# Side work between MoE items, three units' squares on GpSimd, and two reciprocal transfers for four

## The chip, the cores and the metric

One core of a Trainium2 chip runs the whole kernel. The metric is the device time in microseconds (us) of one execution. A kernel is timed in rounds, on the same chip as the kernel before, and the two are compared round by round.

Engines: TensorE (PE in the profile, its weight loads PEld), VectorE (DVE), ScalarE (ACT), GpSimd (POOL), SyncE (SP), whose queue issues most DMAs.

## The reference, cut to what matters

Attention with normalized q and k, 8 batches of 12 heads, 448 tokens, head size 64; its output goes through a two-layer block of width 2048 with a leaky ReLU, which the kernel calls MoE.

```python
def rmsnorm(x, g):
    rms = np.sqrt(np.mean(x * x, axis=-1, keepdims=True) + 1e-06)
    return x / rms * g
# ... q_n, k_n = normalized q, k; scores, softmax (exp, divided by the row sums), times v
h = x @ w_in                  # x: 3584 x 768, w_in: 768 x 2048
g = np.maximum(0.01 * h, h)
return (g @ w_out)            # w_out: 2048 x 768
```

## The kernel before

A unit is four heads of one batch, so there are 24 units and three to a batch. Each unit has four steps, d0 to d3. A step issues scores (`qk`), their exp (`ex`), some side work, and then `fill`, which hands out MoE items from a queue to keep TensorE busy. An item is six first-layer matmuls with a leaky ReLU on ScalarE (`moe1`), or eight second-layer matmuls (`moe2`). The items of a batch are pushed in step d3 of the unit after its last one; the first batch's are pushed early, in unit 2.

The side work of unit u prepares unit u + 2 (squares, sums, inverse norms, norms, a transpose by DMA) and finishes unit u - 1: a reciprocal of the softmax sums on ScalarE, spread over partitions by DMAs into `rz`, and a product on GpSimd that gives `xt`, the input of the first layer.

```python
def zcol_inv(u):                       # reciprocal of the softmax sums
    nc.scalar.activation(s["zs"], s["zs"], AF.Ln)
    nc.scalar.activation(s["zs"], s["zs"], AF.Exp, bias=0.0, scale=-1.0)
    # ...
    for r in range(2):
        for a in range(2):
            src = s["zs"][32 * a + 16 * r:32 * a + 16 * r + 16, None, :]
            nc.sync.dma_start(s["rz"][64 * a:64 * a + 64, r], src.broadcast_to([16, 4, S]))

# in the loop over units u and steps d  (cut)
    ex(u)
    if d == 0:
        # ...
        elif narrow(u - 1):
            zcol_inv(u - 1)            # ScalarE, then SyncE's queue
        # ...
        if u + 4 < NU:
            load(u + 4)                # q and k, 448 KB each, SyncE's queue
        if u + 2 < NU:
            prep_qg(u + 2, nc.gpsimd)
        if u + 3 < NU:
            load_v(u + 3)              # v, 224 KB, issued by GpSimd
        if 3 < u < NU - 2:
            prep_sq(u + 2)             # squares of q and k, ScalarE
    if d == 1 and u > 3 and narrow(u - 1):
        xmul_pool(u - 1)               # the product on GpSimd
    # ... d == 1: sums of squares; d == 2: inverse norms, norms, transpose
    fill(u, d)
```

## Time and profile before

| | |
|---|---|
| time | 452.05 us, 3 runs (451.57 to 452.19); later rounds gave medians of 451.8 to 452.6 |
| span of the profiled run | 450.6 us |
| 12 first-layer matmuls at the second batch's start | 3.45 us (2.37 undisturbed) |
| a unit in the steady part | 16.87 us |
| reciprocal DMAs | 76 of 112 KB, 3.3 us each from issue to landing |

The prediction below shows the lines of the page and of the timeline that carry its argument. What TensorE waits for from 50 us to 440 us stands in the list of waits (engine and line, what it waited for, total us, times, longest us):

```profile
PE sT L179 <- ACT et L198: 5.4, 8, 1.2
...
PE hps L325 <- POOL xt L290: 0.9, 1, 0.9
```

The first line is scores that wait for exp to free a PSUM slot, the second the second batch's first item, which waits for the product on GpSimd.

One more view of the kernel before matters afterwards: how the second batch's wait comes about, in the timeline of unit 6 (start, duration, engine, line, operation; SPq and POOL L106 rows are issues of DMAs):

```profile
93.96 0.76 POOL L106 DMA_DIRECT2D vt<-in_v_dram  x1
...
97.17 0.58 ACT L278 ACTIVATE zs<-zs 64x448 f32<-64x448 f32 x1
97.77 2.92 SPq L283 DMA_DIRECT2D rz<-zs  x4
100.79 0.55 SPq L103 DMA_DIRECT2D rq<-in_q_dram  x1
...
103.62 2.96 POOL L290 TENSOR_TENSOR xt<-x,rz 128x896 f16<-128x896 f32 x1 [8.89 <-ACT rinv L145]
...
106.63 1.67 PE L325 MATMUL hps<-xt,win 128*128 128x448 f16 x8 [0.92 <-POOL xt L290]
```

The load of v is issued 3.8 us before the reciprocal's DMAs, the load of q after them. The reciprocal ends on ScalarE at 97.74, its last DMA lands at 103.36 (5.6 us later, by the trace's record of arrivals), the product follows. (Its bracket names ScalarE's `rinv`, which it doesn't read: that update merely came last.)

### The profile page before, as it was taken

The numbers are of one execution on the slowest core, as the hardware profiler recorded it, in microseconds if no ns is written. First come the engines' busy times: TensorE is split into PE (matmuls) and PEld (weight loads), VectorE is DVE, ScalarE is ACT, GpSimd is POOL, SyncE is SP. The second block draws the span as 40 slices with busy tenths as digits, with TensorE's granted clock in tenths as the row PEclk, the third lists the DMA queues.
The fourth block names the chain that finished last, engine by engine and source line by source line (L and its number), as shares of the span: only waits on it lengthen the run. The fifth ranks groups of instructions, "written<-read, shape, count | busy, mean of one in ns | idle before, by whom it ended". The sixth has DMA issues, their size and how long they took to land.

```text
span 450.6 us, 8689 instructions
## 1 busy us (share of the span) xinstructions
PE 422.9 (94%) x3608; PEld 214.2 (48%) x3608; DVE 216.7 (48%) x320; ACT 313.2 (70%) x464; POOL 142.1 (32%) x96
## 2 busy tenths in 40 slices
PE   6668898889999999999999999999999999999995
PEld 6234343444445544455455544455455544555563
DVE  4688744576354564366354564366354540311011
ACT  5878688866985778966985778966984868444300
POOL 5878333145225135225225135225224101010000
PEclk9578999999999999999999999999999999999999
DMA  8999993777656866677567775587564441321022
GB/s 267 233 242 249 233 213 83 165 124 190 164 92 146 228 131 142 142 141 204 129 97 154 216 135 141 139 149 197 128 99 101 92 92 27 51 61 36 0 71 70
DMA packets 68586, 62.82 MB, mean 139 GB/s; under 512 B 38084, under 2 KB 63428, under 8 KB 68548
## 3 DMA queue, kind: packets, MB, share of 16 engines
q1 hardware_dynamic: 58272, 50.48, 46.3%
q0 software_dynamic: 10272, 11.80, 17.4%
q8 instruction: 28, 0.46, 0.4%
q14 instruction: 10, 0.08, 0.0%
q10 hardware_dynamic: 4, 0.00, 0.0%
HBM read 45.61 MB, written 11.01 MB: 126 GB/s over the span
## 4 chain that ended last, share of the span: by engine, by line
PE 68%; ACT 17%; DVE 7%; DMA 4%; issue 1%; POOL 1%; SPq 1%; DVEq 0%; POOLq 0%
PE op L340 30%; PE hps L325 20%; ACT et L198 7%; PE sT L179 6%; PE sT L310 5%; ACT sq L126 4%; PE zc L255 3%; ACT gt L327 3%; DMA rq<-in_q_dram 2%; ACT zs L277 1%; DVE zs L272 1%; DVE zs L273 1%; DVE ssq L139 1%; ACT zs L278 1%; DMA out_dram<-ost 1%
## 5 line engine op out<-in xcount | busy, mean ns | idle before, releaser
L198 ACT ACTIVATE et<-sT,eb 128x896 f16<-128x896 f32 x166 | 158.3, 1005 | 35.8 <-PE sT L179 25.6
L325 PE MATMUL hps<-xt,win 128*128 128x448 f16 x768 | 154.6, 353 | 2.9 <-DVE xt L319 1.0
L340 PE MATMUL op<-wout,gt 128*128 128x384 f16 x896 | 154.1, 326 | 0.0
L340 PEld LDWEIGHTS <-gt 128*128 128x128 f16 x896 | 84.4, 98 | 65.0 <-issue 11.9
L325 PEld LDWEIGHTS <-win 128*128 128x128 f16 x768 | 72.3, 98 | 74.4 <-issue 12.1
L290 POOL TENSOR_TENSOR xt<-x,rz 128x896 f16<-128x896 f32 x19 | 41.1, 2161 | 202.5 <-DMA rz<-zs 155.2
L327 ACT ACTIVATE gt<-hps 128x448 f16<-128x448 f32 x128 | 63.7, 538 | 21.0 <-PE hps L325 20.4
L134 POOL TENSOR_TENSOR qg<-rq,ggb 128x896 f32<-128x896 f32 (+2 forms) x25 | 64.3, 2573 | 36.5 <-DVE n L151 32.2
L151 DVE TENSOR_TENSOR n<-qg,rinv 128x896 f16<-128x896 f32 (+2 forms) x25 | 31.8, 1276 | 81.0 <-issue 32.9
L179 PE MATMUL sT<-qkT 64*64 64x448 f16 x664 | 54.2, 372 | 11.0 <-ACT et L198 10.5
L139 DVE TENSOR_REDUCE ssq<-sq 128x14 f32<-128x896 f32 (+2 forms) x49 | 50.1, 1061 | 28.9 <-ACT sq L126 28.9
L344 DVE COPY ost<-op 128x384 f32<-128x384 f32 x56 | 30.0, 551 | 58.5 <-PE op L340 58.5
L267 ACT COPY x<-sT 128x896 f32<-128x896 f32 x19 | 17.2, 905 | 32.5 <-PE sT L310 32.5
L179 PEld LDWEIGHTS <-qkT 64*64 64x64 f16 x672 | 15.8, 105 | 47.8 <-issue 44.3
L216 DVE TENSOR_REDUCE sT<-sT 128x1 f32<-128x896 f32 x22 | 24.1, 1095 | 29.0 <-PE sT L179 28.9
L151 DVE TENSOR_TENSOR n<-rk,rinv 128x896 f16<-128x896 f32 (+2 forms) x25 | 29.8, 1195 | 0.0
L310 PE MATMUL sT<-et,vt 64*64 64x448 f16 x532 | 28.5, 349 | 0.3
L310 PEld LDWEIGHTS <-vt 64*64 64x64 f16 x672 | 20.8, 109 | 12.0 <-issue 2.8
L126 ACT ACTIVATE sq<-rq 128x896 f32<-128x896 f32 (+2 forms) x22 | 19.7, 902 | 2.0 <-DMA rq<-in_q_dram 2.0
L126 ACT ACTIVATE sq<-rk 128x896 f32<-128x896 f32 x20 | 18.7, 935 | 0.0
L106 POOL DMA_DIRECT2D vt<-in_v_dram x24 | 18.4, 765 | 0.0
L255 PE MATMUL zc<-et,onesr 128*32 128x448 f16 (+1 forms) x304 | 16.1, 332 | 0.0
(60 smaller groups left out, 191.1 us busy)
## 6 DMA issues: line engine op xcount, KB each, us to landing
rq<-in_q_dram SPq DMA_DIRECT2D x24, 448.0 KB, 4.8
rk<-in_k_dram SPq DMA_DIRECT2D x24, 448.0 KB, 5.4
out_dram<-ost SPq DMA_DIRECT2D x56, 192.0 KB, 4.6
rz<-zs SPq DMA_DIRECT2D x76, 112.0 KB, 3.3
vt<-in_v_dram POOLq DMA_DIRECT2D x24, 224.0 KB, 5.5
win<-in_moe_w_in_dram POOLq DMA_DIRECT2D x8, 384.0 KB, 12.3
wout<-in_moe_w_out_dram POOLq DMA_DIRECT2D x2, 1536.0 KB, 22.1
qkT<-n SPq DMA_TRANSPOSE x19, 4.0
```

What stands on the lines that cost most here:

```text
L126: nc.scalar.activation(buf(u, "sq")[:, ti, :, c[0]:c[1]], raw[u][ti][:, :, c[0]:c[1]], AF.Square)
L134: eng.tensor_tensor(buf(u, "qg")[:, :, c[0]:c[1]], raw[u][0][:, :, c[0]:c[1]], ggb[:, None, None, :].broadcast_to([P, 2, n, D]), op=ALU.mult)
L139: nc.vector.tensor_reduce(buf(u, "ssq")[:, ti, :, c[0]:c[1]], buf(u, "sq")[:, ti, :, c[0]:c[1]], axis=AXL.X, op=ALU.add)
L151: nc.vector.tensor_tensor(buf(u, "n16")[:, ti, c[0]:c[1]].rearrange("p s a d -> p a s d"), src[:, :, c[0]:c[1]], buf(u, "rinv")[:, ti, :, ...
L179: nc.tensor.matmul(banks[a][64 * r:64 * r + 64, 0:S].rearrange("p (t x) -> p t x", t=NS), kT(u, r, a, t), qT(u, r, a), start=True, stop=True)
L198: nc.scalar.activation(s["et"][:, t], sT[:, :, 0:S], AF.Exp, bias=s["eb"], scale=1.0)
L290: nc.gpsimd.tensor_tensor(xts[b][:, g], s["x32"], s["rz"], op=ALU.mult)
L310: nc.tensor.matmul(s["pv"][r][64 * a:64 * a + 64, 0:S], vts[u % NV][64 * r:64 * r + 64, a, t], s["et"][64 * r:64 * r + 64, t, a], start=(t ...
L325: nc.tensor.matmul(hps[:, 0:S], win16[:, kt // 2, kt % 2, ts(ft, P)], xt[:, kt // 2, kt % 2], start=(kt == 0), stop=(kt == KT - 1))
L327: nc.scalar.activation(gt[:, ft, ds(S * (b % 2), S)], hps[:, 0:S], AF.Prelu, bias=0.0, scale=1.0, alpha=0.01)
L340: nc.tensor.matmul(op2[:, 0:HC], gt[:, ft, ts(t, P)], wout16[:, ft, ds(HC * half, HC)], start=(ft == 0), stop=(ft == FT - 1))
L344: nc.vector.tensor_copy(ost[0][:, ds(HC * half, HC)], op2[:, 0:HC])
```

## The change

Its intent: ScalarE and VectorE did a unit's side work in one piece ahead of the items, which held up exps and the emptying of PSUM. The change hands the pieces out one by one between items, takes the squares of units 6 to 8 off ScalarE, and halves the number of reciprocal DMAs by interleaving the rows of the sums.

```diff
-        nc.vector.memset(onesr[64 * r:64 * r + 64, 16 * r:16 * r + 16], 1.0)
+        nc.vector.memset(onesr[64 * r:64 * r + 64].rearrange("p (i r) -> p r i", r=2)[:, r], 1.0)
 ...
-            for a in range(2):
-                src = s["zs"][32 * a + 16 * r:32 * a + 16 * r + 16, None, :]
-                nc.sync.dma_start(s["rz"][64 * a:64 * a + 64, r], src.broadcast_to([16, 4, S]))
+            src = s["zs"][r:64:2, None, :]
+            nc.sync.dma_start(s["rz"][:, r], src.broadcast_to([32, 4, S]))
 ...                                          (in fill, behind each item)
+            if jobs:
+                jobs.pop(0)()
+        for job in jobs:
+            job()
 ...                                          (in the loop)
-                        zcol_inv(u - 1)
+                        job(zcol_inv, u - 1)
 ...
-                    if 3 < u < NU - 2:
-                        prep_sq(u + 2)
+                    if 6 < u < NU - 2:
+                        for ti in range(2):
+                            job(prep_sq, u + 2, ALL, (ti,))
 ...
+                if u < 6 and d == 2:
+                    prep_sqp(u + 3)                      # squares on GpSimd
 ...                                          (sums, inverse norms, norms, transpose: job(...) too)
-                fill(u, d)
+                fill(u, d, jobs)
```

Not shown in the cut: `pv_out`, a copy on ScalarE, and `zcol_sum` on VectorE change places.

More of the change, by code (lines that the diff above doesn't have):

```diff
@@ L372, in fed, with fill @@
         return u % NQ == 0 and d == 3
-    def fill(u, d):
+    def fill(u, d, jobs):
         total = sum(c for c, _ in queue)
@@ L531 @@
                             shift_mm(u)
+                            pv_out(u - 1)
                             zcol_sum(u - 1)
-                            pv_out(u - 1)
                         else:
@@ L539, with job @@
                     ex(u)
+                jobs = []
+                def job(fn, *args):
+                    jobs.append(lambda: fn(*args))
                 if d == 0:
@@ L566 @@
                     if d == 1:
-                        prep_ssq(u + 2)
+                        for ti in range(2):
+                            job(prep_ssq, u + 2, ALL, (ti,))
                     if d == 2:
-                        prep_rinv(u + 2)
-                        prep_norm(u + 2)
-                        prep_trd(u + 2)
-                fill(u, d)
+                        job(prep_rinv, u + 2)
+                        for ti in range(2):
+                            job(prep_norm, u + 2, ALL, (ti,))
+                        job(prep_trd, u + 2)
+                fill(u, d, jobs)
         zsum_slot(NU - 1)
```

## The prediction

> **What bounds the kernel now.** I read the page first, then the timeline unit by unit, then the chain of waits for the rates of undisturbed matmuls, and last the waits and the places where transfers land. A unit is four heads of one batch; each has four steps (d0 to d3): scores into PSUM, their exp on ScalarE, then some MoE items that fill TensorE meanwhile.
>
> ```profile
> PE 422.9 (94%) x3608; PEld 214.2 (48%) x3608; DVE 216.7 (48%) x320; ACT 313.2 (70%) x464; POOL 142.1 (32%) x96
> ...
> PE   6668898889999999999999999999999999999995
> ...
> ACT  5878688866985778966985778966984868444300
> POOL 5878333145225135225225135225224101010000
> ```
>
> TensorE is the bound. Its idle time lies in the first ten slices (11.3 us each), so to 113 us; behind it the row shows nines to the end. The page's busy time hides small stalls, though, so I compare the starts of successive blocks of matmuls in the timeline with undisturbed rates. These are at the end of the chain of waits, where nothing disturbs them:
>
> ```profile
> 406.46 18.16 PE hps L325 x96
> 424.62 20.81 PE op L340 x128
> ```
>
> That is 0.189 us for a first-layer matmul (an item of 6: 1.13 us) and 0.163 us for a second-layer one (an item of 8: 1.30 us). A pair of score steps, 8 matmuls, takes 0.51 us from its start to the next block's in undisturbed places (198.42 to 198.93), and a block of 16 second-layer matmuls with its switch 2.70 us (198.93 to 201.63). What blocks take beyond that is what any better order could win. From 45 us on it is 12.9 us in sum: about 9.0 us between 45 and 115 us (units 3 to 7), and about 3.9 us, in pieces of 0.1 to 0.5 us, from there to the end. The start-up before 45 us isn't touched by the change. The largest pieces all look like this one, in unit 6 (timeline: start, duration, engine, line, operation, and in brackets idle time with its releaser):
>
> ```profile
> 95.25 1.01 ACT L198 ACTIVATE et<-sT,eb 128x896 f16<-128x896 f32 x1 [0.55 <-DVE eb L226]
> ...
> 96.62 2.77 PE L340 MATMUL op<-wout,gt 128*128 128x384 f16 x16
> 97.17 0.58 ACT L278 ACTIVATE zs<-zs 64x448 f32<-64x448 f32 x1
> 97.65 0.94 ACT L126 ACTIVATE sq<-rq 128x896 f32<-128x896 f32 x1
> ...
> 98.49 0.93 ACT L126 ACTIVATE sq<-rk 128x896 f32<-128x896 f32 x1
> ...
> 99.33 3.66 ACT L198 ACTIVATE et<-sT,eb 128x896 f16<-128x896 f32 x4
> 100.36 0.38 PE L179 MATMUL sT<-qkT 64*64 64x448 f16 x4 [0.97 <-ACT et L198]
> ```
>
> The scores of d2 need PSUM slots that the exps of d1 free. Those exps could have started at 97.75, when the reciprocal's second activation ended, but ScalarE first squared q and k, to 99.33. So TensorE stood from about 99.3 to 100.36, and again before the second score step (1.21 us from 100.36 to 101.57 in place of 0.51). The same in units 4 and 5:
>
> | unit | block before d2 | stall | score pair | stall |
> |---|---|---|---|---|
> | 4 | 67.77 to 70.13, 6 matmuls | 1.1 | 70.13 to 71.34 | 0.7 |
> | 5 | 82.27 to 84.92, 8 matmuls | 1.2 | 84.92 to 86.13 | 0.7 |
> | 6 | 96.62 to 100.36, 16 matmuls | 1.0 | 100.36 to 101.57 | 0.7 |
>
> Sum 5.4 us. These are just the units whose d0 squares those of units 6, 7, 8: few items run in d0 there (8 to 16 matmuls, 1.5 to 2.8 us), too little to cover ScalarE's exp, reciprocal and squares (1.0 + 1.2 + 1.7 us). A further 1.1 us is lost at 104.78 to 108.23 (12 first-layer matmuls in 3.45 us in place of 2.37), where the second batch waits for unit 5's product on GpSimd, which itself waits for the reciprocal's DMAs.
>
> **What the skill says.** The Trainium skill, "Perfetto Trace Analysis", § Identifying the Most-Contended Engine, holds that matmul busy time is a poor measure because matmuls are pipelined; the trace agrees: the slice from 210 to 220 us is nearly all busy on the page and still holds a 0.5 us wait for exp. The same page, § Optimizing Scalar/DVE Operations, says that where ScalarE or VectorE isn't saturated but causes bubbles elsewhere, breaking instructions up may let work finish sooner; ScalarE is 70% busy here and causes these, so the intent fits. "GPSIMD Engine Reference", § 3.1, gives about 2.6 cycles an element for a two-input fp32 product; at its 1.2 GHz that would be about 1.9 us for 896 elements, an estimate from that page. This trace has squares on GpSimd at 1.67 us, and I use that. "SBUF — State Buffer", § Who interferes with whom, says that VectorE with two SBUF inputs and a reading GpSimd exclude each other for whole instructions, and whichever comes first blocks the other. The trace agrees:
>
> ```profile
> 88.10 1.09 DVE L151 TENSOR_TENSOR n<-qg,rinv 128x896 f16<-128x896 f32 x1 [2.85 <-issue]
> 88.26 2.87 POOL L290 TENSOR_TENSOR xt<-x,rz 128x896 f16<-128x896 f32 x1 [9.75 <-DMA rz<-zs]
> ...
> 89.11 2.97 DVE L151 TENSOR_TENSOR n<-rk,rinv 128x896 f16<-128x896 f32 x1
> ...
> 91.09 2.93 POOL L134 TENSOR_TENSOR qg<-rq,ggb 128x896 f32<-128x896 f32 x1
> ```
>
> The two engines take turns: a 1.08 us norm becomes 2.97, a 2.07 us product 2.87.
>
> **The change, part by part.**
>
> *Squares of units 6 to 8 to GpSimd.* ScalarE loses 6 squares, each adding 0.84 us in sequence (97.65 to 98.49), so 1.7 us in each of units 4, 5, 6. Unit 4: exp of d0 ends 66.64; the second item's leaky ReLU is ready only at about 67.45, so d1's exps move from 69.06 to about 67.9. Gain 1.1 us, not 1.7. Unit 5: the reciprocal ends 82.30, d1's exps start there, not at 83.88. Gain 1.6 us. Unit 6: from 99.33 to 97.75, again 1.6 us. Together 4.3 of the 5.4 us; the rest stays as about 0.3 to 0.7 us before a second score step.
>
> *Cost on GpSimd.* Six more products of 1.67 us, 10 us on an engine that is 32% busy. In units 3 and 4 they lie in empty time (GpSimd is free from 55.7 to 60.3 and from 63.2 to 74.9). In unit 5 they come right behind the product at 88.26 and on top of unit 7's norms on VectorE. If each norm waits for a GpSimd instruction, the last ends some 1.4 us later against TensorE's progress than now, the shift maximum of unit 6 stands behind it in VectorE's order, and TensorE waits in the shift matmul. If the norm of q gets in first, nothing is lost. I charge half: 0.7 us.
>
> *Two reciprocal DMAs for four.* The 448 KB of a unit stay (4 x 112 KB on the page, now 2 x 224 KB), but there are 38 issues rather than 76. Four issues take 2.9 to 3.0 us on the SyncE queue (0.59 us median plus gaps), two about 1.3 us. If a 224 KB transfer lands in about the 3.3 us that a 112 KB one has on the page, the product on GpSimd starts some 1.3 us earlier. It matters only for unit 5: TensorE now arrives there 1.6 us earlier, its data 1.3 us earlier, so the 1.1 us stall grows to about 1.4: minus 0.3 us. Elsewhere the products wait long (155 us in all for these DMAs), but older items feed TensorE meanwhile.
>
> *Side jobs between items.* No instruction goes away. In a unit of first-layer items, d0 now runs: exp, reciprocal, two squares, then all leaky ReLUs:
>
> ```profile
> 213.53 0.58 ACT L277 ACTIVATE zs<-zs 64x448 f32<-64x448 f32 x1 [0.30 <-DVE zs L273]
> ...
> 216.31 1.80 ACT L327 ACTIVATE gt<-hps 128x448 f16<-128x448 f32 x4
> ...
> 216.88 2.43 PE L325 MATMUL hps<-xt,win 128*128 128x448 f16 x12 [0.17 <-ACT gt L327]
> ...
> 218.00 1.89 ACT L198 ACTIVATE et<-sT,eb 128x896 f16<-128x896 f32 x2
> ```
>
> Interleaved, the PSUM banks come free sooner, so the 0.17 us at 216.88 goes, and ScalarE's 0.30 us wait before the reciprocal is filled. But d1's exps stand behind the same sum of work: from 213.24, four leaky ReLUs 1.80, reciprocal 1.2, squares 1.7 to 1.8 make 218.0, where they start now. The 0.5 us stall at 219.24 keeps most of its size. I take 1.0 of the 3.9 us of small stalls as won. Norms and sums that come one or two items later have a unit of slack before their transpose is used. The strided ones in the row-sum weights cost nothing; swapping the copy of the product and the row sums swaps two engines' instructions, not one engine's order.
>
> Sum: 4.3 - 0.7 - 0.3 + 1.0 = 4.3 us. 452.05 - 4.3 = 447.7 us.
>
> **The rivals.** (1) *The lock between VectorE and GpSimd eats it.* For: the 2.97 us norms above; the shift maximum of unit 6 already starts at 92.93, 0.9 us after its scores start. Against: only one of three pairs of squares meets norms. At its worst 1.4 us plus about 1 us more from unit 3's pair: 449.5. (2) *The chain through the reciprocal becomes the wait.* It is now issued behind the first item, so behind one leaky ReLU where that is first-layer (0.43 us), and the batch's first item waits for it. For: the 1.1 us at 104.78. Against: in units 4 to 6 the first items are mostly second-layer, with no ScalarE work. If the larger DMAs land 1.3 us slower each, unit 6's gain is lost: 449. (3) *Interleaving works better than my sum of ScalarE's work allows*, because the small stalls of 3.9 us and the remaining 1.1 us all go: 452.05 - 4.3 - 3.9 - 1.1 = 442.8, the only way past 2%. Against: it needs ScalarE to do the same work in less time.
>
> **Range and chances.** 2% is 9.0 us, of 12.9 that exist at all; that asks for two thirds of everything, so faster by over 2% gets 0.03. Slower by over 2% needs a new wait of 9 us where the trace shows slack: 0.02. Rivals 1 and 2 together give about 450.6, the upper end; most of the small stalls gone, with no lock cost, about 445, the lower.
>
> **What would show it.** Right: d1's exps in units 4 to 6 start right behind the reciprocal, no 1 us wait of the scores for exp there; GpSimd 10 us busier, ScalarE about 5.6 us less; unit 7's shift maximum (now at 108.74) about 3.3 us earlier, and later units keeping their pace of nearly 16.9 us (in the chain of waits, six units from 144.03 to 245.24). Wrong: TensorE waiting for the shift matmul of unit 6 behind a long norm; a longer wait of the second batch for GpSimd's product; later units each faster by half a us or more, which would say that order within ScalarE counts for more than its sum.

## The result, and the profile after

The changed kernel took 450.1 us, median of 4 runs (449.42 to 450.52), against 451.81 us of the kernel before in the same rounds (451.56 to 452.19). The ratio is 0.996, 95% interval 0.9943 to 0.9977: the same within 2%. It was predicted to be 447.7. A ratio here is the mean time of one kernel's fast runs over that of the other's fast runs of the same rounds, so it isn't quite the ratio of the medians. In a later set of rounds the same kernel had 449.38 us against 452.57 us, ratio 0.9921 (0.9889 to 0.9953).

The page after, its busy times and the rows of slices:

```profile
PE 421.5 (94%) x3608; PEld 213.6 (48%) x3608; DVE 216.4 (48%) x320; ACT 307.4 (69%) x458; POOL 150.0 (34%) x102
...
PE   7477799997999999999999999999999999999995
...
PEclk9688999998999999999999999999999999999999
```

ScalarE lost 5.8 us, as forecast (5.6). GpSimd gained 7.9 us rather than 10, mostly because its `qg` products took 2.4 us less. But in the tenth slice (100.7 to 111.9 us) TensorE is down to 7 tenths, and its granted clock to 8, which the kernel before doesn't show there. The list of waits for 50 us to 440 us has changed places:

```profile
PE hps L324 <- POOL xt L289: 3.2, 1, 3.2
...
PE sT L179 <- ACT et L198: 0.4, 1, 0.4
```

The scores' waits for exp are nearly gone, 5.4 to 0.4 us. The one wait for the product on GpSimd has grown from 0.9 to 3.2 us. Unit 6 in the timeline after:

```profile
90.91 1.05 SPq L103 DMA_DIRECT2D rq<-in_q_dram  x1
...
92.01 0.47 SPq L103 DMA_DIRECT2D rk<-in_k_dram  x1
...
94.01 1.11 SPq L349 DMA_DIRECT2D out_dram<-ost  x2
94.16 0.58 ACT L278 ACTIVATE zs<-zs 64x448 f32<-64x448 f32 x1
94.36 0.76 POOL L106 DMA_DIRECT2D vt<-in_v_dram  x1
94.64 1.88 ACT L198 ACTIVATE et<-sT,eb 128x896 f16<-128x896 f32 x2
95.22 1.22 SPq L282 DMA_DIRECT2D rz<-zs  x2
...
101.34 2.85 POOL L289 TENSOR_TENSOR xt<-x,rz 128x896 f16<-128x896 f32 x1 [6.22 <-DMA rz<-zs]
...
104.24 1.89 PE L324 MATMUL hps<-xt,win 128*128 128x448 f16 x8 [3.21 <-POOL xt L289]
```

Three things read off here. d1's exps at 94.64 stand right behind the reciprocal, as predicted. The loads of q and k (896 KB) are now issued ahead of the reciprocal's DMAs, because those are a job and jobs run inside `fill`, behind the line with the loads. And the load of v, which GpSimd issues in its own order, comes out at 94.36, in the same microsecond as the reciprocal: two squares stand ahead of it on GpSimd now. The two reciprocal DMAs have landed at 101.17, 6.4 us behind the activation's end at 94.74, with half the issues of before.

The matmuls are the same, in the same order, in all kernels but one below, so time between the starts of two given matmuls can be compared directly. Four stretches, in us:

- A: from the shift matmul of unit 3 (48.84 us in the kernel before) to the second batch's first item (104.78). Units 3 to 6.
- B: the 12 first-layer matmuls there, to the next scores (108.23). The second batch's wait.
- C: to the next row sums (109.87).
- D: the rest, to the last matmul's start (445.09).

| kernel | A | B | C | D | sum | reciprocal's end to last landing |
|---|---|---|---|---|---|---|
| before | 55.94 | 3.45 | 1.64 | 335.22 | 396.25 | 5.6 |
| changed, first trace | 51.35 | 5.96 | 3.05 | 333.18 | 393.54 | 6.4 |
| changed, second trace | 51.35 | 5.75 | 1.64 | 334.17 | 392.90 | 6.3 |
| squares only | 51.34 | 4.80 | 1.64 | 335.34 | 393.12 | 5.9 |
| two DMAs only | 55.94 | 2.37 | 1.64 | 335.19 | 395.14 | 4.35 |
| jobs only | 55.94 | 3.54 | 1.64 | 333.18 | 394.30 | 6.7 |
| reciprocal first | 51.35 | 4.74 | 1.64 | 334.99 | 392.72 | 5.9 |
| loads of q, k later | 51.35 | 5.74 | 1.64 | 332.58 | 391.32 | 6.6 |
| four DMAs | 51.35 | 6.13 | 2.88 | 333.12 | 393.49 | 6.4 |
| v early | 51.34 | 4.74 | 1.64 | 333.34 | 391.07 | 5.35 |
| v early, q and k later | 51.34 | 3.27 | 1.64 | 332.59 | 388.84 | 4.8 |
| squares only, v early | 51.35 | 4.80 | 1.64 | 335.32 | 393.10 | 5.6 |
| v early, q and k later, four DMAs | 51.35 | 4.75 | 1.64 | 332.62 | 390.36 | 6.2 |

What stands before A is left out on purpose. Up to that matmul no kernel changes anything on TensorE's way, and yet it took 46.7 to 49.5 us from the first matmul over these traces, with stretches at half the granted clock in other places each time. (The five traces with such a stretch between 41.7 and 42.9 us took 48.5 to 49.5, the nine others at most 47.7.) In one set of rounds the unedited kernel before ran from 450.75 to 454.79 us. So for a microsecond I go by the table more than by a median of six runs. But each row is one trace, and the two of the changed kernel differ by 0.2 us in B, 1.4 in C and 1.0 in D.

### The profile page after: what moved, and what is told of

The parts are those of the page before. It is cut to its first block, busy times and chain, and to the rows that moved or that the text cites. A ratio compares the mean times of both kernels' runs of the same rounds, so it can differ in the third digit from the quotient of the medians.

```text
span 447.6 us, 8612 instructions
## 1 busy us (share of the span) xinstructions
PE 421.5 (94%) x3608; PEld 213.6 (48%) x3608; DVE 216.4 (48%) x320; ACT 307.4 (69%) x458; POOL 150.0 (34%) x102
## 4 chain that ended last, share of the span: by engine, by line
PE 73%; ACT 16%; DVE 7%; issue 1%; DMA 1%; POOL 1%; SPq 0%; POOLq 0%; DVEq 0%
PE op L339 29%; PE hps L324 23%; ACT et L198 8%; PE sT L179 7%; PE sT L309 6%; PE zc L255 3%; ACT gt L326 3%; DVE n L151 2%; ACT sq L126 2%; DVE ssq L139 1%; DMA rz<-zs 1%; PE pb L223 1%; PE pv L309 1%; PE warm L401 1%; ACT zs L278 1%
## 5 line engine op out<-in xcount | busy, mean ns | idle before, releaser
L326 ACT ACTIVATE gt<-hps 128x448 f16<-128x448 f32 x128 | 67.1, 539 | 24.3 <-PE hps L324 23.8
L343 DVE COPY ost<-op 128x384 f32<-128x384 f32 x56 | 31.2, 556 | 102.4 <-PE op L339 99.6
L134 POOL TENSOR_TENSOR qg<-rq,ggb 128x896 f32<-128x896 f32 (+2 forms) x25 | 61.9, 2476 | 33.6 <-DVE n L151 29.2
L151 DVE TENSOR_TENSOR n<-qg,rinv 128x896 f16<-128x896 f32 (+2 forms) x25 | 29.4, 1180 | 38.2 <-ACT rinv L145 32.9
L309 PE MATMUL sT<-et,vt 64*64 64x448 f16 x532 | 29.7, 361 | 0.3
L126 ACT ACTIVATE sq<-rq 128x896 f32<-128x896 f32 (+2 forms) x19 | 16.9, 897 | 1.1 <-DMA rq<-in_q_dram 1.1
L126 ACT ACTIVATE sq<-rk 128x896 f32<-128x896 f32 x17 | 16.0, 940 | 0.0
```

Of the source, the lines that this page charges most:

```text
L126: nc.scalar.activation(buf(u, "sq")[:, ti, :, c[0]:c[1]], raw[u][ti][:, :, c[0]:c[1]], AF.Square)
L134: eng.tensor_tensor(buf(u, "qg")[:, :, c[0]:c[1]], raw[u][0][:, :, c[0]:c[1]], ggb[:, None, None, :].broadcast_to([P, 2, n, D]), op=ALU.mult)
L151: nc.vector.tensor_tensor(buf(u, "n16")[:, ti, c[0]:c[1]].rearrange("p s a d -> p a s d"), src[:, :, c[0]:c[1]], buf(u, "rinv")[:, ti, :, ...
L309: nc.tensor.matmul(s["pv"][r][64 * a:64 * a + 64, 0:S], vts[u % NV][64 * r:64 * r + 64, a, t], s["et"][64 * r:64 * r + 64, t, a], start=(t ...
L326: nc.scalar.activation(gt[:, ft, ds(S * (b % 2), S)], hps[:, 0:S], AF.Prelu, bias=0.0, scale=1.0, alpha=0.01)
L343: nc.vector.tensor_copy(ost[0][:, ds(HC * half, HC)], op2[:, 0:HC])
```

## The experiments

Theory A: the loads of q and k ahead of the reciprocal's DMAs make these land late. Rivals: B, the larger transfers themselves; C, the lock between VectorE and GpSimd; D, the load of v, which the squares on GpSimd hold back until it falls on the reciprocal's DMAs. Twelve runs followed, eleven new kernels and the changed one again; all gave correct results.

### Reciprocal first (e1_recip_first)

```diff
-                        job(zcol_inv, u - 1)
+                        zcol_inv(u - 1)
```

> The changed kernel with one part undone: the reciprocal of a unit (two activations, two DMAs) is issued at its old place, ahead of the loads of q and k, not as a job between items. Theory A (the loads, 896 KB, now go out ahead of the reciprocal's DMAs on the SyncE queue, and those land late): the reciprocal of unit 5 lands about 4 us behind its activation rather than 6.4, the second batch's wait for the product on GpSimd falls from 3.2 us to about 1 to 1.5 us, no stretch at half clock follows near 105 us, and the time is 446.3 to 447.5. Theory B (two DMAs of 224 KB land later than four of 112 KB because of their size): the wait stays near 3 us, the time near 450. Theory C (the lock between VectorE and GpSimd makes the product late): wait falls by under 1 us, time 449 to 450.

449.55 us against 451.78 (ratio 0.9939, 0.9914 to 0.9965). Landing 5.9 us behind the activation, TensorE's wait 2.2 us rather than 3.2, stretch B 4.74 rather than 5.96. The wait falls by half of what theory A claimed, the landing by 0.5 us of 2.4: the loads are clear of the way, but v's 256 packets of 896 bytes run from 97.24 to 99.82 in this trace, and the reciprocal's first DMA, issued at 96.17, lands at 101.2. Another half microsecond of B is the product, which takes 2.37 us rather than 2.85 beside VectorE's norm. The run also lost something: D is 334.99, no better than before. The reciprocal's place between the items is where the later units had gained.

### Loads of q and k later (e2_loads_later)

```diff
-                    if u + 4 < NU:
-                        load(u + 4)
 ...
                 fill(u, d, jobs)
+                if d == 0 and u + 4 < NU:
+                    load(u + 4)
```

> The changed kernel with the reciprocal left as a job between items, but the loads of q and k of unit u + 4 issued behind the items of the first step, so behind the reciprocal's DMAs. Theory A (order on the SyncE queue alone): as good as the run with the reciprocal first, 446.3 to 447.5, wait of the second batch 1 to 1.5 us. If it is the reciprocal's place among ScalarE's work that counts instead, the time stays near 450. Theory B and C: near 450.

449.03 us against 451.78 (0.9925, 0.99 to 0.9949). A miss for theory A alone: the wait stays at 3.2 us and the landing at 6.6 us. An output pair is still issued right ahead of the reciprocal (95.91 to 97.0), and v's packets run from 98.17 to 101.95, across it. What the order does help is D, 332.58, 0.6 us better than the changed kernel's better trace. At unit 12, where a later batch starts, its first 12 matmuls take the undisturbed 2.37 us. In all five traces with the loads ahead of the reciprocal (changed twice, four DMAs, v early, jobs only) they take 2.56 to 3.64, in the eight others that can be compared 2.37. So the loads' place counts there, and the 1.0 us between the D of the changed kernel's two traces is this wait (2.56 and 3.64). B and C as single causes would leave the wait at the second batch too, so they stay.

### Four DMAs again (e3_four_dmas)

```diff
-            src = s["zs"][r:64:2, None, :]
-            nc.sync.dma_start(s["rz"][:, r], src.broadcast_to([32, 4, S]))
+            for a in range(2):
+                src = s["zs"][32 * a + 16 * r:32 * a + 16 * r + 16, None, :]
+                nc.sync.dma_start(s["rz"][64 * a:64 * a + 64, r], src.broadcast_to([16, 4, S]))
```

(with the old memset of the row-sum weights)

> The changed kernel with the old four reciprocal DMAs of 112 KB and the old layout of the row-sum weights; loads still ahead of them. Theory A: the loads are still ahead, so the second batch waits as long as in the changed kernel or some 0.5 to 1.3 us longer (two more issues): 450 to 451.5. Theory B (size of the transfers): the wait falls to about 1.5 us, time 447 to 448.

448.58 us against 451.78 (0.9926, 0.9902 to 0.9949); stretches B 6.13 and C 2.88, landing 6.4 us. The time lies below what was expected, which the start-up's chance may cover (46.77 us in its trace, near the shortest seen); the stretches are as theory A, or any theory of other transfers in the way, wants them. Theory B falls: with the old small DMAs the landing is as late. In this place two DMAs gain nothing over four that the trace shows.

### Squares only (e4_squares_only)

Of the change, only this on the kernel before:

```diff
-                    if 3 < u < NU - 2:
+                    if 6 < u < NU - 2:
                         prep_sq(u + 2)
 ...
+                if u < 6 and d == 2:
+                    prep_sqp(u + 3)
```

> The kernel before with one part of the change alone: squares of units 6 to 8 on GpSimd. The three stalls of 5.4 us in units 4 to 6 shrink to about 0.8 us as in the changed kernel (4.6 us). Theory A: the loads stay behind the reciprocal's DMAs, so these land as long behind their activation as before (5.6 us), and the second batch's wait grows by unit 6's gain only, from 1.1 to about 2.7 us: 448.5 to 449.3, and 450 if the wait sets off a stretch at half clock. Theory C (lock): wait above 3 us and 450 or more, with the product on GpSimd starting late behind the squares.

449.28 us against 451.78 (0.9946, 0.9918 to 0.9974). A falls by 4.60 us, just as in the changed kernel, and B grows by 1.35 us, since TensorE arrives earlier at the same wait. Expected were 4.6 and about 1.6. The lock as theory C has it (a wait above 3 us, a product that starts late behind the squares) doesn't show: the product starts 0.26 us behind the last landing.

### The changed kernel again (r_changed)

No edit.

> The changed kernel again, unedited, so that it shares its rounds with the runs beside it and a second trace shows what repeats. All theories: 449.4 to 450.5; the second batch's wait near 6 us for its 12 matmuls. If the stretch at half clock behind that wait is chance (windows of 3.4 us that start where they will), this trace may lack it.

449.38 us against 452.57 (0.9921, 0.9889 to 0.9953). The wait of 3.2 us repeats; the stretch at half clock behind it doesn't. Instead the same kind of wait comes once more, at unit 12, where 12 first-layer matmuls at 204.92 take 3.64 us rather than the 2.37 of the kernel before.

### v early (e5_v_early)

```diff
-                    if u + 3 < NU:
+                    if u + 3 < NU and u not in (4, 5, 6):
                         load_v(u + 3)
 ...
                 if u < 6 and d == 2:
+                    load_v(u + 4)
                     prep_sqp(u + 3)
```

> The changed kernel with one move: the loads of v for units 7 to 9, which GpSimd issues, stand ahead of the squares on GpSimd rather than behind squares and gain product. Theory D (the squares hold back GpSimd's load of v, 224 KB, until it falls on top of the reciprocal's DMAs; packets of the reciprocal start only when those of v end): the reciprocal of unit 5 lands some 5 to 5.5 us behind its activation rather than 6.4, the 12 matmuls of the second batch take 4.5 to 5.2 us rather than 5.96, and the time falls by about 1 us to 448.8 to 449.3. Theory A (loads of q and k ahead on the SyncE queue): nothing changes, 450.

447.19 us against 452.57 (0.9891, 0.9861 to 0.992), against 449.38 of the changed kernel in the same rounds. Landing 5.35 us, B 4.74. Theory D holds for its share, 1.0 to 1.2 us of B, though not in its strict form: in the changed kernel the reciprocal's packets start at 98.08, while v's run to 100.17. The time fell by more than B; the table gives 1.8 to 2.5 us between the traces. The rest lies in C and D, where the changed kernel's own two traces differ.

### v early, loads of q and k later (e6_v_early_loads_later)

Both edits above together.

> Both transfers out of the reciprocal's way: loads of v ahead of the squares and loads of q and k behind the reciprocal's DMAs, all else as changed. Theories A and D together: the reciprocal lands within about 4.5 us of its activation, the 12 matmuls take 3.4 to 4.2 us, no stretch at half clock, and the time is 446.5 to 447.5, which the prediction gave. If a third thing holds the reciprocal up (outputs on the SyncE queue ahead of it), the 12 matmuls stay above 5 us and the time above 448.5.

444.45 us, six runs from 443.83 to 446.06, against 452.57 (0.9824, 0.9796 to 0.9852), and against 449.38 of the changed kernel in the same rounds. Unit 6:

```profile
94.40 1.22 SPq L282 DMA_DIRECT2D rz<-zs  x2
...
95.72 0.69 SPq L103 DMA_DIRECT2D rq<-in_q_dram  x1
...
98.82 2.08 POOL L289 TENSOR_TENSOR xt<-x,rz 128x896 f16<-128x896 f32 x1 [5.21 <-DMA rz<-zs]
...
100.96 1.68 PE L324 MATMUL hps<-xt,win 128*128 128x448 f16 x8 [0.74 <-POOL xt L289]
```

The reciprocal's DMAs land 4.8 us behind the activation, TensorE waits 0.74 us where it waited 3.21. Neither edit alone got more than 1.2 us out of B; together they get 2.5 to 2.7. Each load stood in the way by itself, so clearing one left the other. The product takes 2.08 us here and 2.85 in the changed kernel: landing earlier, it also escapes the norm on VectorE (101.18 to 102.26 there), which is theory C's share of 0.8 us. In six traces where a norm was still running when the product started (before, changed, e1, e4, e5, e7), the product is longer than 2.07 us by what was left of the norm less some 0.14 us: by 0.29 with 0.42 left in e4, by 0.89 with 1.02 left in the kernel before. So of the 2.7 us that B lost against the first trace of the changed kernel, landing is 1.7 (1.1 with v early, 0.6 more with q and k later), the lock 0.8, and half clock the rest. This is the best version found, and it beats both kernels; whether by 2% against the kernel before is unclear by the interval.

### Squares only, v early (e7_squares_v_early)

The e4 kernel with the v edit.

> The kernel before with the squares of units 6 to 8 on GpSimd (as in the run with that part alone) and the loads of v for units 7 to 9 ahead of them. Theory D: the 12 matmuls of the second batch fall from 4.80 us to 3.5 to 4.2 us and the time by about 1 us against the run with squares alone, to 448.2 or so. Theory A or lock alone: 4.8 us as there.

450.35 us against 452.57 (0.9946, 0.9917 to 0.9975). A miss: B is 4.80 us, as without the edit, though v had landed by 93.9, before the reciprocal's end at 94.2. With four DMAs the issues alone take until 97.13 and the last lands 2.7 us later, as in the kernel before. There, v cost little of the landing, the four issues most: it came at 5.6 us rather than 5.9, and the product gave those 0.3 us back (2.64 us rather than 2.36), because starting earlier it met more of VectorE's norm.

### Jobs only (e8_jobs_only)

The changed kernel with four DMAs and with the squares of units 6 to 8 on ScalarE, as jobs.

```diff
-                    if 6 < u < NU - 2:
+                    if 3 < u < NU - 2:
 ...
-                if u < 6 and d == 2:
-                    prep_sqp(u + 3)
```

> The kernel before with one part of the change alone: side work issued as jobs between items (squares of units 6 to 8 stay on ScalarE, as jobs too), four reciprocal DMAs. If the jobs are what wins in the later units: from the second batch's first item to the end some 2 to 2.5 us less than before (335.2 us from the same matmul on), as in the changed kernel. Units 3 to 6, where ScalarE still squares: 58.5 to 59.5 us for a stretch of 59.48 before, since the exps of the next step stand behind the same work. The loads now go out ahead of the reciprocal: the second batch waits as long as before or 1 us longer. Time 449.5 to 451, against some 452 before.

452.28 us against 452.39 (0.9981, 0.9947 to 1.0014), with the longest start-up of all in its trace. D falls by 2.04 us, A doesn't move by 0.01 us: in units 4 to 6 interleaving wins nothing, because the exps wait for the same work. The reciprocal lands 6.7 us behind its activation, so the job costs 1.1 us there. B grows by 0.09 us only, since the product now starts ahead of the norm and takes 2.07 us rather than 2.96.

### Two DMAs only (e9_two_dmas_only)

The kernel before with the two DMAs and the interleaved rows.

> The kernel before with two reciprocal DMAs of 224 KB in place of four of 112 KB. The prediction's step: landing 1.3 us earlier behind the activation (5.6 us before). What the pairs of runs so far suggest: 0 us where other transfers stand in the way, up to 0.8 us where the queue is clear; here outputs of unit 5's items stand ahead, so 0.3 to 0.8 us, and the 12 matmuls of the second batch take 2.6 to 3.2 us rather than 3.45. Time within 1 us of before.

450.96 us against 452.39 (0.9976, 0.9945 to 1.0007).

```profile
97.58 1.22 SPq L282 DMA_DIRECT2D rz<-zs  x2
...
102.08 2.07 POOL L289 TENSOR_TENSOR xt<-x,rz 128x896 f16<-128x896 f32 x1 [8.79 <-ACT et L198]
```

Landing 4.35 us behind the activation, 1.27 us less than before, and B is 2.37, all of the wait gone. My own expectation of 0.3 to 0.8 us was too low; the prediction's 1.3 us was right, for the kernel before.

### Items kept back (e10_items_kept_back)

```diff
-        left = WD[d] + 1.0
+        left = WD[d] + (4.0 if u < 7 else 1.0)
```

on the best kernel.

> The best kernel so far (loads of v early, loads of q and k behind the reciprocal) with a slower hand-out of items up to unit 6, so that two second-layer items of the first batch are still queued when the second batch's are pushed. TensorE then has 2.6 us of work while it waits for unit 5's product: the stall of 0.9 us at the second batch's first items is gone, nothing else changes. Time about 1 us less than that kernel: 443.3 to 444. If the stall only moves to an earlier step (fewer items to cover ScalarE in units 3 to 6), no gain.

448.03 us against 452.39 (0.991, 0.9878 to 0.9943), worse than the best kernel. B's matmuls no longer wait, but the items' order has changed, and a lock that the prediction feared comes up:

```profile
87.69 2.56 DVE L151 TENSOR_TENSOR n<-rk,rinv 128x896 f16<-128x896 f32 x1
...
90.17 1.08 DVE L216 TENSOR_REDUCE sT<-sT 128x1 f32<-128x896 f32 x1
91.29 0.29 DVE L218 TENSOR_TENSOR dg<-ident,sT 128x128 f16<-128x128 f16 x1
91.63 0.22 PE L223 MATMUL pb<-dg,onesp 128*128 128x128 f16 x1 [1.93 <-DVE dg L218]
```

The norm of k is stretched to 2.56 us beside the squares on GpSimd, the shift maximum starts at 90.17 although its scores started at 86.87, and TensorE waits 1.93 us in the shift matmul. Later units lost as well: D can't be compared matmul by matmul here, but scores wait 1.9 us for exp in all, against 0.4.

### Four DMAs with a clear way (e11_four_dmas_clear)

The best kernel with the four DMAs of e3.

> The same best kernel with four reciprocal DMAs of 112 KB instead of two of 224 KB, while no load stands in the way. If two issues save time only when the queue is clear: landing 0.8 to 1.3 us later behind the activation than the 4.8 us with two, the 12 matmuls 4.0 to 4.6 us rather than 3.27, time about 1 us more, 445.5. If the number of DMAs never matters: 3.3 us and 444.5.

446.91 us against 452.39 (0.9872, 0.9843 to 0.9901). Landing 6.2 us, B 4.75 rather than 3.27. Two DMAs for four are worth 1.4 to 1.5 us where the way is clear, and nothing where it isn't (e3).

## Why the prediction was wrong

Its time was 447.7 us, the measured 450.1. Step by step, from the two traces of the changed kernel:

1. *Squares to GpSimd, 4.3 us.* Right: A fell by 4.59 us, and alone by 4.60.
2. *Lock on unit 6's shift maximum, 0.7 us lost.* Not there. The norm of q got in ahead of GpSimd's product (85.22 against 85.81), the branch in which the prediction loses nothing. The maximum started 0.55 us behind its scores, and A has the full gain. The rival was a real mechanism all the same, as e10 shows with 1.93 us.
3. *Two DMAs land 1.3 us earlier, so unit 5's wait grows by 0.3 us only.* **This step failed.** It added the DMAs' gain (1.27 us, measured alone) to a landing that the rest of the change makes later. The prediction took the job's place to move only ScalarE's work, by one leaky ReLU at most, and looked for the cost of the squares only on VectorE. It didn't follow the two queues: in SyncE's the loads of q and k pass the reciprocal, in GpSimd's the load of v falls behind the squares. The landing came 6.3 to 6.4 us behind the activation rather than about 4.3, and B grew by 2.3 to 2.5 us rather than 0.3. e5 and e6 show both transfers as causes; e3 and e11 show that behind them the two DMAs' gain is nil. The 2.1 us between 6.4 and the 4.35 us of two DMAs alone are 1.1 for v (e5), 0.6 for q and k (e6 after e5), and 0.4 for a pair of outputs that is issued just ahead: the reciprocal's first DMA then goes out 0.5 us behind the activation's end, and 0.02 us behind it in e9 and e10, where no pair stands there and the landing comes after 4.35 and 4.33 us.

   Rival 2 named this very wait, and the sign "a longer wait of the second batch for GpSimd's product" came true, but not for the causes it gave. The activation ends 5.36 us ahead of the batch's first item with the job (changed) and without it (e4), and the larger DMAs alone land earlier. That 450.1 lies inside the stated range, near the end that rivals 1 and 2 make together, is therefore luck.
4. *Small stalls, 1.0 of 3.9 us.* Too low: D fell by 2.04 us in one trace and with the jobs alone, and by 1.05 in the other trace with its new wait at unit 12. e1 shows that most of it comes from the reciprocal behind the first item. (One reading was loose: of the 0.49 us that TensorE idles from 200 to 220 us, 0.32 is a wait for exp, not 0.5; 0.17 is the wait at 216.88.)
5. *Not in the sum:* the long wait once set off 3.4 us at half clock, which cost 1.4 us in C.

With the parts alone: squares -4.60 and +1.35, two DMAs -1.08, jobs -2.04 and +0.09, together -6.3 us. The changed kernel has -2.7 and -3.3. The 2.9 to 3.6 us between are B's extra 1.9 to 2.2 us, and 1.4 us of half clock or 1.0 us in D, one in each trace. Every part does what the prediction says or better; their meeting on the DMA queues, with what it sets off, takes about half of it back.

Between the traces' 2.7 to 3.3 us and the 1.7 us between the first medians a difference is left; the later rounds gave 3.2. The start-up differs by more than that from run to run, but the timed runs without a trace don't show theirs, so this stays an explanation that is possible and not shown. Open too is why taking the loads of q and k away alone gained nothing in e2, with v still in the way: that the slower of two obstacles hides the other fits all runs, and isn't shown directly.

## What to carry to other kernels

When an instruction moves in program order, follow it in every queue that it or its dependents use: here a job on ScalarE took its DMAs behind 896 KB of loads, and two squares on GpSimd pushed a load that GpSimd issues onto the transfer that mattered. Parts that each gain when tried alone can share one waiting transfer, so look at what lands last when they are together. And before a microsecond is believed, compare traces from the same matmul on, because the start-up may vary by more (2.9 us here).

## What the Trainium skill lacked or had wrong

- "TensorE: Matmul & The Clock Gate", § HAM oscillation — how this bites in real kernels, puts the rule as no idle gaps above about 3.4 us. Here TensorE idled 3.2 us, and in two of the four traces with such a wait (changed, four DMAs) the granted clock fell to half for 3.4 us, from 1.2 to 1.3 us behind the wait's end, at a cost of 1.2 to 1.4 us; in the other two (changed again, loads later) it didn't. So shorter gaps can be enough. The free-running window of 3413 ns in that page's § What's actually happening agrees: within a trace the half-clock stretches start whole multiples of 3.413 us apart (40.71, 105.56 and 446.90 us in the changed kernel: 19 and 100 of them). On this grid, the window that held most of the wait held 2.09 and 2.26 us of it where the clock fell, 1.95 and 1.83 where it didn't. Where the wait falls on the grid may decide, then; four traces don't show it.
- "DMA: Bandwidth & Descriptors", § Issuing engines are not separate DMA queues, calls the sequencer's time to initiate a DMA usually small relative to the DMA itself. Here four issues took 2.9 us of the 5.6 us from activation to last landing, and two for four gave 1.3 to 1.5 us. Its statement that DMAs of all issuing engines interleave on the same 16 DMA engines agrees: v's load from GpSimd delayed SyncE's transfers by about 1 us.
- No page names it as a cost to plan for that a load issued by GpSimd waits behind compute instructions in GpSimd's order: here the squares moved it from 3.8 us ahead of the reciprocal's DMAs to 0.9 us ahead (0.2 us with the squares alone).
